# Keys in three chunks of 128 and a rest of 64 instead of four chunks of 112, in an attention and SwiGLU kernel

## The chip, the cores and the metric

The kernel runs on one core of one Trainium2 chip. The time is the device time of one launch in microseconds (us), and the median of several runs is given. Engines are named as the profile names them: PE is TensorE with its matmuls, PEld its weight loads, DVE VectorE, ACT ScalarE, POOL GpSimd. A trailing q marks an engine's own queue of issues.

## The reference

Attention over 8 sequences of 448 tokens and 12 heads of 64, whose result, rearranged to 3584 x 768, goes through a SwiGLU block. All in float32; only the weights of the second block arrive as float64.

```python
def rmsnorm(x, g):
    return x / np.sqrt(np.mean(x * x, axis=-1, keepdims=True) + 1e-06) * g
q_n, k_n = rmsnorm(q, g_q), rmsnorm(k, g_k)              # (8, 12, 448, 64)
scores = (1 / np.sqrt(64)) * np.matmul(q_n, k_n.transpose(0, 1, 3, 2))
attn = np.exp(scores - np.max(scores, axis=-1, keepdims=True))
attn = attn / (np.sum(attn, axis=-1, keepdims=True) + 1e-09)
x = np.matmul(attn, v)  # -> transposed to (3584, 768)
xn = rmsnorm(x, rms_g)
g, val = xn @ w_gate, xn @ w_val                          # (3584, 1536) each
return (g / (1 + np.exp(-g)) * val) @ w_out               # (3584, 768)
```

## The kernel before

The kernel works through 48 pairs of heads, g = 0 to 47, six for each sequence. The keys of a pair lie in NT = 4 chunks of P = 112 tokens, and the scores are held transposed: keys on the partitions, the 448 queries along the row. Four steps on PE belong to a pair.

`turn` transposes the four chunks, both heads side by side (112 rows, 128 columns), so that head 0 lies on partitions 0 to 63 and head 1 on 64 to 127:

```python
def turn(g, i):                      # i = 0: the normalized q, i = 1: k
    ...
    ps = (ps_m if todo else ps_f).tile([128, 512], F32, name="tr", ...)
    for t in range(NT):
        nc.tensor.transpose(ps[:, t * P:(t + 1) * P], src[:, t * 2 * D:(t + 1) * 2 * D], ident[0:P, 0:P])
```

`score` multiplies the keys of one chunk by the queries. The two heads use the two row halves of the array and run at the same time, and ACT makes the exponentials:

```python
def score(g, cs):
    for c in cs:
        for j in range(2):
            r = slice(j * D, (j + 1) * D)
            ps = sc[c, j] = ps_s.tile([128, 512], F32, name="sc", tag="s")
            nc.tensor.matmul(ps[0:P, 0:S], lhsT=qkT[r, 1, c * P:(c + 1) * P], rhs=qkT[r, 0, :], start=True, stop=True)
    for (c, j), ps in sc.items():
        e = st["e", g, c, j] = e_pool.tile([P, S], F32, name="e")
        nc.scalar.activation(e, ps[0:P, 0:S], ACT.Exp, scale=rs[:, n:n + 1])
```

`values` multiplies the exponentials by v, one head on each column half, and `sums` does the same with ones in place of v, for the denominators. For the first seven pairs, g = 0 to 6, PE sums all chunks itself (`direct`); later POOL adds the chunks up first and PE sums one tile per head:

```python
def values(g):
    av = st["av", g] = ps_m.tile([128, 512], F32, name="av", tag="m")
    for c in range(NT):
        for j in range(2):
            nc.tensor.matmul(av[j * D:(j + 1) * D, 0:S], lhsT=vt[:, j, c, :], rhs=st["e", g, c, j],
                             start=(c == 0), stop=(c == NT - 1))

def sums(g):
    den = ...
    terms = [[st["e", g, c, j] ...]] if direct(g) else [[st["es", g, j] for j in range(2)]]
    for i, pair in enumerate(terms):
        for j, term in enumerate(pair):
            nc.tensor.matmul(den[j * D:(j + 1) * D, 0:S], lhsT=ones[0:P, :], rhs=term, ...)
    ...   # reciprocal of den; x = av * reciprocal, on DVE
```

The PSUM banks come from three pools: four for scores, one for `av`, three for the matmuls of the second block. The transposes take one of these three in the early part and the one of `av` later on. Pairs 1 to 6 run back to back. From pair 7 on, an attention block is set between stretches of the second block's matmuls (`ff`, always the full 128 x 128 array), which `fill` issues:

```python
if g < NG:
    pe(lambda: score(g, (0, 1)))
pe(lambda: values(g - 1))
...
pe(lambda: sums(g - 1))
...
    pe(lambda: score(g, (2, 3)))
...
fill(); squares(g + 2, 0); squares(g + 2, 1)
pe(lambda: turn(g + 1, 0)); fill(); pe(lambda: turn(g + 1, 1)); fill()
```

## Time and profile before

| | before |
|---|---|
| median of 3 runs | 1627.66 us (1627.48 to 1628.2) |
| span of the profiled run, granted clock | 1625.3 us, 0.999 |
| first matmul of the second block starts | 95.8 us |
| from there to the end | 1529.5 us |
| one attention block in the steady part | 7.31 us |
| one turn (four transposes) | 0.385 us |

The first two rows are as measured. The others are differences of starts in PE's timeline. That is the way to read PE: it is busy 99% of the span and the ends of its matmuls are modelled, but a start is where work really begins, and from one group's start to the next one's start nothing is lost or counted twice. The lines that carry this are in the prediction.

### The profile page before, as it was taken

What the parts mean: (1) busy time and instruction counts of PE and PEld (TensorE: products, weight loads), DVE (VectorE), ACT (ScalarE), POOL (GpSimd) and SP (SyncE); (2) the same over time, 40 slices, a digit from 0 to 9 for tenths busy, and PEclk for the clock granted to TensorE, in tenths of its full rate; (3) what the DMA queues carried; (4) which work ended last, traced back from release to release, by engine and by line L of the source; (5) the groups of instructions that cost most, each with busy time, mean ns of one, the idle gap of its engine ahead of it and who ended that gap; (6) DMA issues with size and microseconds to landing.
All of it is one profiled execution on the core that took longest, in us unless ns stands there. A gap on an engine that the chain in (4) does not pass through costs nothing.

```text
span 1625.3 us, 21571 instructions
## 1 busy us (share of the span) xinstructions
PE 1608.9 (99%) x7376; PEld 1139.7 (70%) x7376; DVE 871.2 (54%) x1425; ACT 500.3 (31%) x975; POOL 632.2 (39%) x569
## 2 busy tenths in 40 slices
PE   8999999999999999999999999999999999999998
PEld 4444445678855888568865788658786588969974
DVE  6989898487842555335572354624565234433431
ACT  7856563232222332232232222322332123100110
POOL 7777776343523434244334323434343223100000
PEclk9999999999999999999999999999999999999999
DMA  8756674666855555565544655466454453557651
GB/s 223 208 176 200 183 219 134 217 222 200 267 183 154 164 154 156 166 197 154 155 120 131 201 155 147 120 215 194 130 163 132 147 176 108 152 182 239 175 148 45
DMA packets 249036, 276.83 MB, mean 170 GB/s; under 512 B 66644, under 2 KB 245844, under 8 KB 248916
## 3 DMA queue, kind: packets, MB, share of 16 engines
q1 hardware_dynamic: 248596, 275.34, 56.7%
q8 instruction: 61, 1.00, 0.3%
q14 instruction: 59, 0.48, 0.1%
q10 hardware_dynamic: 320, 0.00, 0.0%
HBM read 235.93 MB, written 39.32 MB: 169 GB/s over the span
## 4 chain that ended last, share of the span: by engine, by line
PE 91%; DVE 5%; DMA 2%; ACT 1%; issue 0%; POOL 0%; SPq 0%; DVEq 0%; ACTq 0%; POOLq 0%
PE ff L797 41%; PE ff L991 21%; PE sc L476 9%; PE av L501 9%; PE den L512 3%; PE ff L892 3%; PE ff L1022 2%; PE tr L461 2%; DVE top L646 1%; DVE top L645 1%; DVE rd L520 1%; DVE top L644 1%; DMA raw<-in_moe_w_out_dram 0%; ACT e L480 0%; PE rb L558 0%; DMA raw<-in_moe_w_val_dram 0%
## 5 line engine op out<-in xcount | busy, mean ns | idle before, releaser
L797 PE MATMUL ff<-x,w 128*128 128x224 f32 x1770 | 359.3, 353 | 0.8 <-DVE u L809 0.8
L797 PEld LDWEIGHTS ff<-x,w 128*128 128x128 f32 x1770 | 332.2, 190 | 9.8 <-issue 6.7
L797 PE MATMUL ff<-xs,w 128*128 128x224 f32 x1326 | 272.3, 353 | 0.4 <-DVE cc L809 0.4
L480 ACT ACTIVATE e<-sc,rs 112x448 f32<-112x448 f32 x384 | 212.1, 638 | 190.2 <-PE sc L476 185.2
L486 POOL TENSOR_TENSOR es<-e 112x448 f32<-112x448 f32 x82 | 95.3, 1184 | 436.1 <-ACT e L480 436.0
L797 PEld LDWEIGHTS ff<-xs,w 128*128 128x128 f32 x1326 | 248.6, 190 | 6.1 <-issue 5.3
L490 POOL TENSOR_TENSOR es<-es,e 112x448 f32<-112x448 f32 x164 | 185.9, 1144 | 85.4 <-ACT e L480 78.9
L991 PE MATMUL ff<-w,h 128*128 128x384 f32 x600 | 203.4, 488 | 0.0
L520 DVE RECIPROCAL rd<-rd 128x448 f32<-128x448 f32 x41 | 121.1, 2953 | 135.9 <-ACT rd L519 135.9
L476 PE MATMUL sc<-qkT 64*112 64x448 f32 x768 | 176.7, 562 | 1.6 <-DVE qkT L466 0.8
L991 PEld LDWEIGHTS ff<-w,h 128*128 128x128 f32 x600 | 112.3, 190 | 78.6 <-issue 4.7
L501 PE MATMUL av<-e,vt 112*64 112x448 f32 x768 | 154.9, 545 | 0.0
L444 POOL TENSOR_TENSOR rs<-ms,mhalf 112x16 f32<-112x16 f32 (+1 forms) x50 | 143.7, 2874 | 4.2
L476 PEld LDWEIGHTS sc<-qkT 64*112 64x112 f32 x768 | 68.8, 172 | 93.2 <-issue 69.5
L991 PE MATMUL ff<-w,so 128*128 128x384 f32 x338 | 116.7, 488 | 2.0 <-DVE y L952 2.0
L501 PEld LDWEIGHTS av<-e,vt 112*64 112x64 f32 x768 | 50.8, 136 | 95.8 <-issue 73.9
L1022 PE MATMUL ff<-x,w 128*128 128x448 f32 x288 | 112.0, 542 | 0.0
L809 DVE TENSOR_TENSOR cc<-ff,u 128x448 f32<-128x448 f32 x84 | 52.3, 623 | 93.3 <-PE ff L797 93.0
L991 PEld LDWEIGHTS ff<-w,so 128*128 128x128 f32 x338 | 63.2, 190 | 46.5 <-DVE y L952 3.9
L427 DVE TENSOR_REDUCE ms<-sq 112x8 f32<-112x512 f32 x96 | 61.3, 678 | 52.0 <-ACT sq L424 51.7
L682 POOL TENSOR_TENSOR w<-top,raw 128x384 int32<-128x384 int32 x72 | 78.0, 1097 | 28.3 <-DVE top L646 13.4
L1022 PEld LDWEIGHTS ff<-x,w 128*128 128x128 f32 x288 | 53.3, 190 | 50.9 <-issue 49.0
(104 smaller groups left out, 1676.2 us busy)
## 6 DMA issues: line engine op xcount, KB each, us to landing
w<-kept SPq DMA_DIRECT2D x480, 192.0 KB, 3.2
w<-kept_o SPq DMA_DIRECT2D x290, 192.0 KB, 2.8
kept<-w SPq DMA_DIRECT2D x94, 192.0 KB, 3.7
top<-kept SPq DMA_DIRECT2D x72, 192.0 KB, 3.0
qk<-in_q_dram SPq DMA_DIRECT2D x48, 224.0 KB, 3.6
qk<-in_k_dram SPq DMA_DIRECT2D x96, 112.0 KB, 3.5
vt<-in_v_dram SPq DMA_DIRECT2D x48, 224.0 KB, 2.8
raw<-in_moe_w_gate_dram SPq DMA_DIRECT2D x24, 384.0 KB, 4.7
```

What stands on the lines that cost most here:

```text
L427: nc.vector.tensor_reduce(out=ms[:, i * n:(i + 1) * n], in_=sq.rearrange("p (n d) -> p n d", d=D), axis=AX_X, op=ALU.add)
L444: nc.gpsimd.tensor_tensor(st["rs", g][:, cols], ms, mhalf[0:P, cols], ALU.pow)
L476: nc.tensor.matmul(ps[0:P, 0:S], lhsT=qkT[r, 1, c * P:(c + 1) * P], rhs=qkT[r, 0, :], start=True, stop=True)
L480: nc.scalar.activation(e, ps[0:P, 0:S], ACT.Exp, scale=rs[:, n:n + 1])
L486: nc.gpsimd.tensor_tensor(es, st["e", g, 0, j], st["e", g, 1, j], ALU.add)
L490: nc.gpsimd.tensor_tensor(es, es, st["e", g, c, j], ALU.add)
L501: nc.tensor.matmul(av[j * D:(j + 1) * D, 0:S], lhsT=vt[:, j, c, :], rhs=st["e", g, c, j], start=(c == 0), stop=(c == NT - 1))
L520: nc.vector.reciprocal(rd, rd)
L682: nc.gpsimd.tensor_tensor(data(key).bitcast(I32), top, lo, ALU.add)
L797: nc.tensor.matmul(bank[:, w * HT:(w + 1) * HT], lhsT=wt[:, c * 128:(c + 1) * 128], rhs=x[:, c, :], start=onto is None and w == c == 0, st ...
L991: nc.tensor.matmul(ps, lhsT=a, rhs=data(("wo", b, name, c)), start=first and c == 0, stop=c == NFP - 1, skip_group_check=True)
L1022: nc.tensor.matmul(bank[w][:, 0:S], lhsT=data(key)[:, c * 128:(c + 1) * 128], rhs=st["x", 0, half][:, c, :], start=half == c == 0, stop=ha ...
```

## The change

112 rows use 7/8 of the array's rows. The change takes keys in three full chunks of 128 and a rest of 64 (3 x 128 + 64 = 448). A rest needs only a quarter of the array: 64 rows by 64 columns. Two heads' score rests and two heads' value rests are four such quarters, and the intent is that they run side by side, so that a pair takes 3 + 3 + 1 units of streaming instead of 4 + 4. For this a head's rest is written to the other head's half (`across`), and the score rests of pair g are issued together with the value rests of pair g - 1.

The core of the diff; cut are the loads of q and k (two and three per pair instead of one and two, and two more for v), POOL's adds and powers, the stores of the output, and the order of the first seven pairs. There, in pairs 2 to 6, the turns stand ahead of the values before and after the change, but only one chunk of scores goes ahead of them now instead of two:

```diff
+NK, REST = 3, S - 3 * 128
+    qks = [qk_pool.tile([128, 2, 2 * NT * D], F32, name=f"qk{i}") for i in range(4)]
+    for t in qks:
+        nc.vector.memset(t[REST:128, 0].rearrange("p (h n) -> p h n", h=2)[:, :, NK * D:], 0.0)
+        nc.vector.memset(t[REST:128, 1, 2 * NK * D:], 0.0)
+    def own(j):
+        return slice(j * D, (j + 1) * D)
+    def across(j):
+        return own(1 - j)
 ...
     def turn(g, i):
         for t in range(NT):
-            nc.tensor.transpose(ps[:, t * P:(t + 1) * P], src[:, t * 2 * D:(t + 1) * 2 * D], ident[0:P, 0:P])
+            n = 128 if t < NK else REST
+            nc.tensor.transpose(ps[:, t * 128:t * 128 + n], src[0:n, t * 2 * D:(t + 1) * 2 * D], ident[0:n, 0:n])
 ...
+    def rests(g):
+        if g < NG:
+            qkT = st["qkT", g]
+            ps = ps_s.tile([128, 512], F32, name="sc", tag="s")
+            for j in range(2):
+                nc.tensor.matmul(ps[across(j), 0:S], lhsT=qkT[own(j), 1, NK * 128:S], rhs=qkT[own(j), 0, :], start=True, stop=True)
+        if g:
+            vt, e = st["v", g - 1], st["e", g - 1, "rest"]
+            av = st["av", g - 1] = ps_m.tile([128, 512], F32, name="av", tag="m")
+            for j in range(2):
+                nc.tensor.matmul(av[own(j), 0:S], lhsT=vt[across(j), 2 * NK * D:], rhs=e[across(j), :], start=True, stop=False, ...)
+            if direct(g - 1):
+                den = ...      # the same with ones[across(j), :] for vt
 ...
-        if g < NG:
-            pe(lambda: score(g, (0, 1)))
+        pe(lambda: (rests(g), score(g, (0,)) if g < NG else None))
         pe(lambda: values(g - 1))
 ...
         pe(lambda: sums(g - 1))
 ...
-            pe(lambda: score(g, (2, 3)))
+            pe(lambda: score(g, (1, 2)))
```

## The prediction

> **What bounds the kernel now.** I read four views in this order: the page's busy shares, its chain of work that ended last, the groups by form, and the timeline of the matmul engine, because each narrows the one before. First the page:
>
> ```profile
> PE 1608.9 (99%) x7376; PEld 1139.7 (70%) x7376; DVE 871.2 (54%) x1425; ACT 500.3 (31%) x975; POOL 632.2 (39%) x569
> ...
> PE 91%; DVE 5%; DMA 2%; ACT 1%; issue 0%; POOL 0%; SPq 0%; DVEq 0%; ACTq 0%; POOLq 0%
> ```
>
> The matmul engine (PE) is busy 99% of the span and makes 91% of the chain that ended last. Its ends are modelled, so I checked with starts: in the stretch from 300 us on it is one matmul stream with waits of a microsecond at most. So a microsecond of PE work taken out or put in is a microsecond of time, and what ACT, POOL or DMA gain counts only where PE waits for them. The groups by form name the work that the change touches:
>
> ```profile
> L476 PE MATMUL sc<-qkT 64*112 64x448 f32 x768 | 176.7, 562 | 1.6 <-DVE qkT L466 0.8 <-ACT qkT L464 0.7
> L501 PE MATMUL av<-e,vt 112*64 112x448 f32 x768 | 154.9, 545 | 0.0
> L461 PE MATMUL tr<-ident,qn 112*128 112x112 f32 x192 | 26.8, 261 | 2.4 <-POOL qn L448 2.4
> ```
>
> "64*112" is rows by columns of the array. A float32 matmul leaves two records: 768 records are 384 matmuls, eight for each of 48 pairs of heads. PE waited 1.6 us in all before the scores and 0.0 before the values. One pair in the steady part, from the timeline of PE (start, duration, work):
>
> ```profile
> 617.59 2.43 PE L797 MATMUL ff<-x,w 128*128 128x224 f32 x12
> 619.86 2.43 PE L797 MATMUL ff<-xs,w 128*128 128x224 f32 x12
> 622.23 1.76 PE L476 MATMUL sc<-qkT 64*112 64x448 f32 x8
> 623.92 3.23 PE L501 MATMUL av<-e,vt 112*64 112x448 f32 x16
> 626.98 0.92 PE L512 MATMUL den<-es,ones 112*64 112x448 f32 x4
> 627.83 1.78 PE L476 MATMUL sc<-qkT 64*112 64x448 f32 x8
> 629.54 2.54 PE L797 MATMUL ff<-x,w 128*128 128x224 f32 x12
> 631.91 2.43 PE L797 MATMUL ff<-xs,w 128*128 128x224 f32 x12
> 634.18 2.43 PE L797 MATMUL ff<-x,w 128*128 128x224 f32 x12
> 636.46 0.55 PE L461 MATMUL tr<-ident,qn 112*128 112x112 f32 x4
> 636.84 2.45 PE L797 MATMUL ff<-x,w 128*128 128x224 f32 x12
> ```
>
> Three numbers come from the differences of starts. (a) Streaming: 12 records of 224 columns take 2.27 us where nothing changes (617.59 to 619.86), so 0.189 each and about 0.376 for a record of 448 columns, 0.753 for such a matmul. The values' 16 records take 3.06 us (623.92 to 626.98), eight record times and 0.05: the two heads, on the two column halves, run at the same time. So I count in units: one unit is a pair of matmuls side by side, 0.753 us. (b) A change of shape: the 12 records before the scores take 2.37 instead of 2.27, and the 12 after them 2.37 again (629.54 to 631.91). Scores of two units take 1.69 us, not 1.51. So leaving one shape costs about 0.09 (the drain), and entering 128 or 112 columns another 0.09 to 0.10 (first weights not loaded ahead); entering 64 columns costs 0.05. Values to sums, the same shape, costs nothing more. (c) The transposes between ff work, 112*128, show none of it: 634.18 to 636.46 is 2.28, and the four take 0.38. 112 rows and 128 rows are the same shape to the array, 64 rows are not.
>
> **What the Trainium skill says.** "TensorEngine Tiling (Array Packing)", Key Properties: tiles load weights and multiply in parallel, but "Changing tiling mode (not just tile) drains the TensorE". The trace agrees, at 0.09 a drain. The same page, 64×64 Mode (4 tiles), ties a tile to its partitions: SBUF 0-63 to PSUM 64-127 is tile 2, SBUF 64-127 to PSUM 0-63 is tile 8. No instruction of the kernel before uses this mode. "PSUM — Partial Sum Buffer", PSUM bank collisions: row tiles must not write the same bank and quadrant at once. The two rests share a bank but not a quadrant, so by that page they may run together; no run here shows it yet. "FP8 and Floating Point Precision", TensorE Precision Notes: true FP32 is four passes; 448 columns in 0.753 us fit that at 2.4 columns a ns.
>
> **The change, part by part.**
>
> *Score and value streaming: 0.* Before, a pair of heads has 4 units of scores and 4 of values. After, 3 and 3, and the rests. The intent is that the four rest matmuls lie on four quarters and cost one unit, which would make 7 of 8. But follow the operands. Scores of head 0 read rows 0-63 and write partitions 64-127: tile 2. Scores of head 1: rows 64-127 to 0-63, tile 8. Values of head 0 read the other half, rows 64-127, and write 0-63: tile 8. Values of head 1: tile 2. So both pairs want the same two quarters, and the other two stay empty. The rests cost two units, and 3 + 3 + 2 is 8 as before. The 7 early pairs that sum directly on PE have 3 + 1 units of sums for 4: again none saved.
>
> *Order of shapes in a steady pair: +0.15 us.* Before, PE goes ff, scores, values and sums, scores, ff: four changes. After: ff, rests (64*64), scores (64*128), values and sums (128*64), scores, ff: five. The block before is 1.69 + 3.06 + 0.85 + 1.71 = 7.31. After: rests 0.05 + 1.51 + drain 0.09 = 1.65, scores 0.75 + 0.10 + 0.09 = 0.95, values 2.31, sums 0.85, scores 1.70: 7.46.
>
> *The transposes: +0.37 us each, the largest term.* A turn has three of 128 rows now and one of 64 rows. Columns streamed are 3 x 128 + 64 = 448, as 4 x 112 were, so 0.38 us stays. But the last has 64 rows and 128 columns, the form of the scores, not that of its neighbours. I take it to change the mode twice: in, 0.09 drain and 0.10 weights; out, 0.09 and 0.09. That is 0.37 for a turn, and two turns a pair: +0.74.
>
> *Sum of the steady part.* Pairs 7 to 47, some 40 with both turns: 40 x (0.15 + 0.74) = +36 us, all on PE, which never waits there.
>
> *The first seven pairs, about +1.* The two pairs shown by the windows take 11.31 us on PE, with DVE busy 10.8 and 11.1 of it. There scores run 16 records in 4.24 us instead of 3.2, as they wait for PSUM banks that ACT has to empty; spreading the scores takes away this 1.05. New: three more changes in the order of the rests, values and sums (about 0.5) and three by the turns (0.55). PE comes out near 11.3, the vector engine could not go under 11, so -1 to +3 us for six pairs.
>
> *Off the path.* ACT runs 7 exponentials for 8 in a pair, 0.5 us less, at 31% busy: nothing. POOL has six adds as before and one short power: nothing. DMA moves the same bytes; packets of 1024 bytes of q and v become 768 and 256, 1344 become 1664 a pair, +15,000 on 249,036; eight loads a pair are issued for four. The profile shows no wait of PE on these. The stores of the output come in fewer pieces, off the path too.
>
> *Start: +0.5 to +1.* Eight fills of the unused halves ahead of the first loads, more loads to issue (0.4 to 0.6 us each on the queue), a power more before the first exponential of the rest, against one exponential less.
>
> Sum: 36 + 1 + 1 = 38, so 1627.7 + 38 is about 1665 us.
>
> **Rivals.** First, *the four rests do run at once*, as intended: then 48 x 0.753 = 36 us of streaming is saved and, with the terms above, the time is about 1629. Against it stand the partitions of the operands; for it only the intent. If the turns also cost nothing, 1593. Second, *the 64-row transpose does not change the mode*, or its drain is hidden: then only the 0.15 and the ends remain, 6 + 2, and the time is about 1636. Nothing in the trace has a transpose of 64 rows; for the drain speaks that scores with the same rows pay it on each entry. Third, *the rests of two heads do not overlap*, because they write one bank from two row tiles: two units more, 48 x 1.5 = 72 us on top, near 1735. The page on PSUM speaks against it. Fourth, *DVE or DMA becomes the bound* in the stretch of weight conversion (81 to 285 us, DVE 80 to 97% busy): PE has more work now, so the others get slack; this could only swallow some of the added cost, by a few us, as PE waits 1.6 us there now.
>
> **Range and chances.** I give the transposes' mode change about 70%, and its size 25 to 34 us. That holds the time from 1652 to 1675. The second rival pulls to 1636, so the low end goes there; noise at the start and in the early pairs sets the top at 1682. The 2% mark is 1660.2, below my middle but inside the range, so: slower by over 2% 0.58, within 2% 0.38, faster by over 2% 0.04.
>
> **What would show it.** In the timeline of PE after: a turn that takes 0.7 to 0.8 us from its first start to the next ff start and lengthens the ff group before or after it (right), or 0.38 (wrong). Rests whose score and value records start one unit apart, not within 0.02 us of each other; the attention block at about 7.45 us. ACT, POOL and DMA shares lower or the same, PE still about 99%. Early pairs at 11.0 to 11.8 us. The prediction is wrong if the turns cost no more than before, if value rests start together with score rests, or if a wait of PE on ACT, DVE or DMA of over 5 us in total appears.

## The result

| | before | after |
|---|---|---|
| median | 1627.93 us (4 runs) | 1676.12 us (4 runs, 1675.45 to 1678.09) |
| ratio (95%) | | 1.0298 (1.028 to 1.0316): slower |
| span of the profiled run, granted clock | 1625.3 us, 0.999 | 1673.6 us, 0.996 |

A ratio here is the mean time of one kernel's fast runs over the mean of the other's fast runs of the same rounds, so it is not quite the ratio of the quoted medians. The result is correct. The change costs 48.2 us where 38 were predicted, inside the range.

The chain of work that ended last, on the page of the changed kernel; the shares are of the span, and a shape is not told apart in it:

```profile
PE 80%; DVE 2%; DMA 2%; issue 0%; POOL 0%; ACT 0%; SPq 0%; DVEq 0%; ACTq 0%
```

PE is still all but alone on it. The shares add up to 84%: the chain, laid out in order of time, could be followed back to 241.5 us only, so it says nothing about the early part. The groups by form of the changed kernel show what is new on PE, with count, busy time, mean of one, and PE's idle time before the group:

```profile
L502 PE MATMUL sc<-qkT 64*128 64x448 f32 x576 | 139.5, 579 | 3.7 <-ACT e L541 2.9 <-DVE qkT L492 0.8
L526 PE MATMUL sc<-qkT 64*64 64x448 f32 x192 | 47.3, 570 | 0.8 <-ACT qkT L490 0.7
...
L487 PE MATMUL tr<-ident,qn 64*128 64x64 f32 x48 | 13.2, 274 | 0.0
```

576 + 192 score records are the 768 of before: the number of matmuls is the same. The transposes of the rest are a form of their own, 64*128, as the prediction said they would be. What a form costs is not in this view, since matmuls that overlap and matmuls that do not have the same mean; that is in the starts. One steady pair in PE's timeline of the changed kernel:

```profile
650.79 0.97 PE L526 MATMUL sc<-qkT 64*64 64x448 f32 x4
651.60 0.92 PE L531 MATMUL av<-e,vt 64*64 64x448 f32 x4
652.45 1.02 PE L502 MATMUL sc<-qkT 64*128 64x448 f32 x4
653.40 2.48 PE L549 MATMUL av<-e,vt 128*64 128x448 f32 x12
655.70 0.92 PE L562 MATMUL den<-es,ones 128*64 128x448 f32 x4
656.55 1.80 PE L502 MATMUL sc<-qkT 64*128 64x448 f32 x8
658.28 2.54 PE L848 MATMUL ff<-x,w 128*128 128x224 f32 x12
...
662.93 2.43 PE L848 MATMUL ff<-x,w 128*128 128x224 f32 x12
665.20 0.70 PE L487 MATMUL tr<-ident,qn 128*128 128x128 f32 x4
665.82 2.54 PE L848 MATMUL ff<-x,w 128*128 128x224 f32 x12
668.20 0.85 PE L597 MATMUL msx<-ones,ss 128*112 128x1 f32 x8
```

The score rests start at 650.79 and the value rests 0.81 later, the first scores 0.85 after that: two units, one after the other. The block from 650.79 to 658.28 is 7.49 us, where it was 7.31. The turn runs from 665.20 to 665.82, 0.62 us instead of 0.38, and the 12 `ff` records after it take 2.38 (665.82 to 668.20), where 12 between two `ff` groups take 2.27. (The line of a turn names the shape of its first transposes only.)

The whole of PE, cut into kinds of work by starts and summed, in us; the columns of three experiments are used further down:

| work on PE | before | after | full turn | alternating | both |
|---|---|---|---|---|---|
| until the first `ff` matmul | 95.8 | 105.3 | 104.2 | 103.4 | 101.4 |
| `ff` | 1187.2 | 1196.3 | 1191.2 | 1196.6 | 1191.3 |
| turns (80 from here on) | 31.0 | 51.6 | 36.9 | 51.3 | 36.6 |
| scores | 137.4 | 109.7 | 110.6 | 109.2 | 110.1 |
| score and value rests | – | 66.9 | 66.9 | 37.4 | 37.5 |
| values | 127.5 | 94.5 | 94.5 | 94.5 | 94.5 |
| sums | 35.1 | 38.0 | 39.2 | 40.1 | 40.5 |
| norm of x | 11.3 | 11.4 | 11.4 | 11.4 | 11.5 |
| span | 1625.3 | 1673.6 | 1654.9 | 1644.0 | 1623.2 |

After the first `ff` matmul the change costs 38.9 us (1529.5 to 1568.4): turns 20.6, `ff` 9.1, and the attention work 9.1 (300.0 to 309.1). Before that point it costs 9.5 us, where some 2 were predicted.

These 9.5 have three places. **The start**: the scores of pair 1 begin at 20.72 instead of 16.09, +4.6. ACT's first lines with data, of the kernel before:

```profile
4.01 0.63 ACT L424 ACTIVATE sq<-qk 112x512 f32<-112x512 f32 x1 [1.73 <-DMA qk<-in_q_dram]
```

and of the changed kernel:

```profile
6.26 1.15 ACT L445 ACTIVATE sq<-qk 128x512 f32<-128x512 f32 x2 [3.84 <-DMA qk<-in_k_dram]
```

The first squares start 2.25 us later. The clock differs too: in the changed kernel it is at half from 10.72 to 17.54 us, and before the change it was full from 4.48 us on. The score rests of pair 0 take 1.69 us there (12.74 to 14.43), where 0.80 is usual. How much of the 4.6 us the clock makes, no run here settles. **Pairs 1 to 6** take 2.4 us more in all. **The hand-over** from pair 6 to the second block takes 16.61 us instead of 14.12 to 14.19, some 2.4 more. Here is that stretch, with busy time and number of instructions of PE, PEld, DVE, ACT, POOL, then granted clock, DMA share and GB/s, before:

```profile
81.66:95.78 14.12, 14.12 (x72) 6.21 (x73) 10.31 (x13) 7.94 (x16) 12.19 (x11) 1.00 0.63 196
```

and after:

```profile
88.64:105.25 16.61, 14.63 (x70) 5.87 (x68) 7.23 (x10) 7.38 (x14) 9.69 (x11) 0.90 0.54 159
```

PE waits 1.98 us in it (16.61 less 14.63), and its clock averages 0.90. PE's timeline of the changed kernel there:

```profile
92.54 1.71 PE L531 MATMUL av<-e,vt 64*64 64x448 f32 x4 [1.98 <-issue]
93.98 1.76 PE L536 MATMUL den<-e,ones 64*64 64x448 f32 x4
95.67 1.19 PE L502 MATMUL sc<-qkT 64*128 64x448 f32 x4
```

and DVE's timeline of the changed kernel at the same time:

```profile
88.82 2.96 DVE L566 RECIPROCAL rd<-den 128x448 f32<-128x448 f32 x1 [1.67 <-PE den L562]
91.81 0.62 DVE L577 TENSOR_TENSOR x<-av,rd 128x448 f32<-128x448 f32 x1
```

There is one PSUM bank for `av`. The value rests of pair 6 must write it, and DVE frees it with the product that ends at 92.43, behind a reciprocal of 2.96 us. The value rests start 0.11 us later. "issue" in the brackets means that the profile found no releaser; the two views side by side show it. Before, the values stood behind a whole score group, which covered this time. After the wait PE's clock is at half for about 3.4 us: the value rests take 1.44 us from start to start (92.54 to 93.98) and the sums' rests 1.69, instead of 0.75 to 0.85. The clock's part can be read from the experiment own below: it has the same order and the same wait of 1.98 us here, but no half clock, and takes 14.97 us for the stretch (88.59 to 103.56). So about 1.6 of the 2.4 us come with the half clock, which follows this wait in four of the eleven profiles that have it.

### The profile page after: what moved, and what is told of

Same layout as the page of the kernel before. It is cut to its first block, busy times and chain, and to the rows that moved or that the text cites. A ratio compares the mean times of both kernels' runs of the same rounds, so it can differ in the third digit from the quotient of the medians.

```text
span 1673.6 us, 21741 instructions
## 1 busy us (share of the span) xinstructions
PE 1649.7 (99%) x7376; PEld 1143.5 (68%) x7376; DVE 874.7 (52%) x1433; ACT 478.7 (29%) x927; POOL 658.0 (39%) x617
## 4 chain that ended last, share of the span: by engine, by line
PE 80%; DVE 2%; DMA 2%; issue 0%; POOL 0%; ACT 0%; SPq 0%; DVEq 0%; ACTq 0%
PE ff L848 39%; PE ff L1046 20%; PE sc L502 5%; PE av L549 5%; PE ff L943 3%; PE tr L487 2%; PE sc L526 2%; PE av L531 2%; PE den L562 2%; DMA w<-kept_o 1%; DVE w L805 0%; PE ff L1077 0%; DMA w<-kept 0%; PE rb L609 0%; DVE rd L570 0%
## 5 line engine op out<-in xcount | busy, mean ns | idle before, releaser
L513 POOL TENSOR_TENSOR es<-e 128x448 f32<-128x448 f32 x82 | 94.1, 1147 | 598.4 <-ACT e L506 595.2
L506 ACT ACTIVATE e<-sc,rs 128x448 f32<-128x448 f32 x288 | 162.2, 633 | 70.3 <-PE sc L502 69.2
L465 POOL TENSOR_TENSOR rs<-ms,mhalf 128x16 f32<-128x16 f32 (+1 forms) x50 | 143.4, 2869 | 4.2
L502 PE MATMUL sc<-qkT 64*128 64x448 f32 x576 | 139.5, 579 | 3.7 <-ACT e L541 2.9
L549 PE MATMUL av<-e,vt 128*64 128x448 f32 x576 | 118.8, 548 | 0.0
L502 PEld LDWEIGHTS sc<-qkT 64*128 64x128 f32 x576 | 54.4, 188 | 86.8 <-issue 73.7
L515 POOL TENSOR_TENSOR es<-es,e 64x448 f32<-64x448 f32 x82 | 94.9, 1157 | 6.4
L514 POOL TENSOR_TENSOR es<-es,e 128x448 f32<-128x448 f32 x82 | 94.3, 1150 | 6.4
L448 DVE TENSOR_REDUCE ms<-sq 128x8 f32<-128x512 f32 x96 | 61.3, 678 | 53.8 <-ACT sq L445 53.8
L549 PEld LDWEIGHTS av<-e,vt 128*64 128x64 f32 x576 | 37.1, 136 | 76.2 <-issue 74.9
L1077 PEld LDWEIGHTS ff<-x,w 128*128 128x128 f32 x288 | 53.3, 190 | 51.6 <-issue 49.0
```

Source lines behind the costliest of these rows:

```text
L448: nc.vector.tensor_reduce(out=ms[:, i * n:(i + 1) * n], in_=sq.rearrange("p (n d) -> p n d", d=D), axis=AX_X, op=ALU.add)
L465: nc.gpsimd.tensor_tensor(st["rs", g][:, cols], ms, mhalf[:, cols], ALU.pow)
L502: nc.tensor.matmul(ps[:, 0:S], lhsT=qkT[r, 1, c * 128:(c + 1) * 128], rhs=qkT[r, 0, :], start=True, stop=True)
L506: nc.scalar.activation(e, ps[:, 0:S], ACT.Exp, scale=rs[:, n:n + 1])
L513: nc.gpsimd.tensor_tensor(es, st["e", g, 0, j], st["e", g, 1, j], ALU.add)
L514: nc.gpsimd.tensor_tensor(es, es, st["e", g, 2, j], ALU.add)
```

## The experiments

All twelve gave correct results. Times are medians of four or five runs, with the kernel before in the same rounds. A difference to the changed kernel compares runs of different rounds (the experiments ran on three chips); the medians of the kernel before in these differ by up to 1.2 us, so such a difference is good to 1 or 2 us.

### Full turn: the last transpose with 128 rows

Part of the change undone: the fourth transpose takes all 128 rows (the unused half is zeros) and stays in the shape of its neighbours.

```diff
-            n = 128 if t < NK else REST
-            nc.tensor.transpose(ps[:, t * 128:t * 128 + n], src[0:n, ...], ident[0:n, 0:n])
+            nc.tensor.transpose(ps[:, t * 128:(t + 1) * 128], src[:, ...], ident)
```

> The changed kernel with one edit: the fourth transpose of a turn takes all 128 rows and 128 columns of identity (the lower rows are zeros), so that a turn never leaves the 128x128 mode. Theory (mode changes cost): the turn's run goes from 623 ns to about 440 (four times 107 to 110), the first record after it loses its 0.09 us, so some 0.27 us for each of 80 turns in the steady part: -22 us, and -0 to -3 in the early pairs: 1650 to 1655 us against 1676. Rival (the turn is dearer because of its three 128-column transposes, or by waits, not by the mode): the edit adds 64 columns to each turn, so +0.05 us x 94 = +5 us: about 1681.

Measured: 1655.49 us, ratio to before 1.016 (1.0143 to 1.0177), 20.6 less than the changed kernel. PE's timeline of this kernel:

```profile
657.40 2.43 PE L847 MATMUL ff<-x,w 128*128 128x224 f32 x12
659.67 0.60 PE L486 MATMUL tr<-ident,qn 128*128 128x128 f32 x4
660.11 2.44 PE L847 MATMUL ff<-x,w 128*128 128x224 f32 x12
662.38 0.86 PE L596 MATMUL msx<-ones,ss 128*112 128x1 f32 x8
```

The turn takes 0.44 us (659.67 to 660.11) though it streams 64 columns more than the changed one's 0.62, and the `ff` group after it takes 2.27 again (660.11 to 662.38). In the table, turns fall by 14.7 and `ff` by 5.1. So the 64 rows cost these 20 us. That it is a change of mode is read from the starts: in the changed kernel the transposes of one turn start at 665.20, 665.31, 665.42 and 665.62 and the next `ff` record at 665.82, so the longer steps are those into and out of the 64-row one; here all four steps are 0.11.

### Alternating: rests of odd pairs on swapped halves

The disputed cost taken away by itself. In every second pair a head's rest stays on its own half, so that the score rests of pair g and the value rests of pair g - 1 lie on all four quarters.

```diff
+    def swap(g):
+        return g % 2
+    def on(g, j):
+        return own(j ^ swap(g))
 # the score rest; v's load, the adds, the scale column of the exponential likewise with on(g, j)
-                nc.tensor.matmul(ps[across(j), 0:S], lhsT=qkT[own(j), 1, NK * 128:S], ...)
+                nc.tensor.matmul(ps[on(g, j), 0:S], lhsT=qkT[own(j), 1, NK * 128:S], ...)
 # the value rest, and the sums' rest likewise
-                nc.tensor.matmul(av[own(j), 0:S], lhsT=vt[across(j), 2 * NK * D:], rhs=e[across(j), :], ...)
+                nc.tensor.matmul(av[own(j), 0:S], lhsT=vt[on(g - 1, j), 2 * NK * D:], rhs=e[on(g - 1, j), :], ...)
```

> The changed kernel with one edit: pairs with an even number keep a head's rest on its own half, odd ones on the other half, so that the score rests of a pair and the value rests of the pair before lie on four different quarters. Results stay right. Theory (in the changed kernel both pairs of rests ask for the same two quarters, and that alone makes them two units): value records start within 0.02 us of score records, the rests take 0.9 us instead of 1.65, 41 x 0.75 = -31 us in the steady part and up to -4 in the early pairs: 1641 to 1645 us. Rival (four quarters do not run at once for float32, or the array takes only two streams): no change, 1674 to 1678.

Measured: 1646.71 us, ratio 1.0109 (1.0092 to 1.0126), 29.4 less than the changed kernel, a little over the 1641 to 1645 expected. PE's timeline of this kernel:

```profile
638.89 0.59 PE L533 MATMUL sc<-qkT 64*64 64x448 f32 x2
638.90 0.59 PE L538 MATMUL av<-e,vt 64*64 64x448 f32 x2
639.32 0.54 PE L533 MATMUL sc<-qkT 64*64 64x448 f32 x2
639.33 0.54 PE L538 MATMUL av<-e,vt 64*64 64x448 f32 x2
639.80 1.02 PE L509 MATMUL sc<-qkT 64*128 64x448 f32 x4
```

Score and value rests start 0.01 us apart, and all four are done in 0.91 us (638.89 to 639.80), where the changed kernel takes 1.66 (650.79 to 652.45). That is the unit of 0.75 the change was after. The shared quarters, not the idea of quarters, stood in its way.

### Own: every rest on its own half

The rival to "two rests on one quarter": that the crossing to the other half is what costs. The edit of alternating, but in every pair a head's rest stays on its own head's half, so nothing crosses and two rests again want one quarter.

```diff
     def swap(g):
-        return g % 2
+        return 0
```

> Control for the alternating one: every pair keeps a head's rest on its own half, so both pairs of rests lie on the diagonal quarters instead of the other two. Theory (only sharing a quarter counts, not which quarter): no change, 1674 to 1678 us, rests 1.65 us. Rival (the crossed quarters are slower in themselves): the rests get shorter, and the time falls by up to 31 us.

Measured: 1672.68 us, ratio 1.0266 (1.0249 to 1.0283). PE's timeline of this kernel:

```profile
647.99 0.97 PE L533 MATMUL sc<-qkT 64*64 64x448 f32 x4
648.79 0.92 PE L538 MATMUL av<-e,vt 64*64 64x448 f32 x4
```

The rests are one after the other again, 0.80 apart. Which half they use does not matter, only that two want the same. From the first `ff` matmul on this kernel takes 1567.4 us, the changed one 1568.4. Its other 1.7 us lie in the early part (103.6 instead of 105.3), where it shows no stretch of half clock near 92 us; its profiled run came out below what was expected mostly for that reason.

### Both: full turn and alternating together

> The full 128-row fourth transpose and the alternating halves together. Theory (two separate costs on the matmul engine, each paid in full): the two gains add, 1676.1 - 20.6 - 29.4 = 1626 us, as fast as the kernel before (1628 to 1629) within 0.3%. Rival (the early pairs or the weight conversion on the vector engine take over as the bound once the matmul engine has less to do): 1631 to 1640.

Measured: 1626.07 us, ratio 0.9988 (0.9975 to 1.0002). The two effects add up: by the medians 20.6 + 29.4 = 50.0, and 1676.1 to 1626.1 is 50.1; by the ratios to before, 0.0138 + 0.0189 = 0.0327, and 0.0310 measured. So they are separate causes. With them the kernel is level with the one before, not faster. The table tells where the unit saved is spent: after the first `ff` matmul this kernel needs 1521.8 us, 7.7 less than before, with 17.4 less of attention work (300.0 to 282.6), 5.6 more of turns and 4.1 more of `ff`; until then it needs 5.6 more.

### Fills later: the eight fills behind the first loads

The first suspect for the start: the fills of the unused halves stand ahead of `ones` on DVE, and ACT's first work waits for `ones`.

```diff
-    for t in qks:          # at the head of the kernel
-        nc.vector.memset(...); nc.vector.memset(...)
+    for t in qks:          # after the constants
+        nc.vector.memset(...); nc.vector.memset(...)
```

> The changed kernel with its eight fills of the unused halves moved behind the fill of the ones. First scores now start at 12.74 us against 9.91 before the change, the second pair's at 20.72 against 16.09. Theory (the fills hold up the fill of the ones, ACT's first square waits for it, and the small loads of the gains that ACT issues after it hold up the squares): first square of q at 4.0 to 4.5 us instead of 6.26, first scores near 10.5, total -2 to -3 us. Rival (the start is late because a pair has eight loads to issue instead of four, about 0.6 us each): first square 0 to 0.5 us earlier and total -0.5 us or less.

Measured: 1675.45 us, ratio 1.0278 (1.026 to 1.0295), against 1.0298: no gain that the intervals show. They are too wide to exclude the theory's 2 to 3 us (the four runs go from 1672.59 to 1677.53, and the profiled one is the slowest); the profile shows no gain. ACT's timeline of this kernel:

```profile
4.49 0.63 ACT L442 ACTIVATE sq<-qk 128x512 f32<-128x512 f32 x1 [2.22 <-DMA qk<-in_q_dram]
...
14.47 0.63 ACT L442 ACTIVATE sq<-qk 128x512 f32<-128x512 f32 x1 [1.54 <-DMA qk<-in_k_dram]
15.00 0.62 ACT L538 ACTIVATE e<-sc,rs 128x448 f32<-128x448 f32 x1
```

The first square starts at 4.49, near the 4.01 of before, and PE's first scores at 10.97 instead of 12.74. But the first exponential runs at 15.00, where it ran at 14.85 in the changed kernel: ACT takes its work in order, and ahead of it stand squares of the third pair, which wait for a load. What was gained is lost at the next thing in the queue. The clock is a second cause that this run does not separate: it is at half from 9.01 to 26.08 us here, and the 12 score records after the first rests take 6.29 us (12.66 to 18.95), where the changed kernel takes 4.05 (14.43 to 18.48).

### Start: third pair's squares behind the first exponentials

Fills later, the third pair loaded before v, and its squares behind pair 0's exponentials.

```diff
-    load_v(0)
     load_pair(2)
+    load_v(0)
-    squares(2, 0)
-    squares(2, 1)
 ...
             pe(lambda: rests(0))
             pe(lambda: score(0, (0, 1, 2)))
+            squares(2, 0)
+            squares(2, 1)
```

> The changed kernel with only the start altered: the eight fills behind the fill of the ones, the loads of the third pair ahead of the loads of v, and the squares of the third pair behind the exponentials of the first on ACT. The run with the fills alone had first scores 1.8 us earlier and no gain, as ACT then waited until 14.5 us for the third pair's loads before the first exponential. Theory (the start is set by loads issued one by one at 0.6 us each and by squares that stand ahead of the exponentials in ACT's queue): first exponential near 12.5 us instead of 14.85, second pair's scores near 18 instead of 20.7, total -2 to -3.5 us: 1672.5 to 1674. Rival (the early pairs are paced by DVE and POOL, so an earlier start is given back before the first ff): 0 to -1 us.

Measured: 1674.89 us, ratio 1.0291 (1.0277 to 1.0305): within the noise of the changed kernel. The first exponential now starts at 12.81, but the scores of pair 1 only at 20.31 (20.72 in the changed kernel). DVE's timeline of this kernel:

```profile
18.35 1.28 DVE L445 TENSOR_REDUCE ms<-sq 128x8 f32<-128x512 f32 x2 [7.06 <-ACT sq L442]
19.55 0.62 DVE L489 COPY qkT<-tr 128x448 f32<-128x448 f32 x1
```

The copy of pair 1's keys, which these scores need, stands behind the reduces of the third pair's squares, which now come late. DVE sat idle for 7.06 us before them. The wait went from ACT's queue to DVE's.

### Hand-over: two chunks of scores ahead of the rests of pair 7

```diff
+        if g == NPAIR + 1:
+            pe(lambda: (score(g, (0, 1)), rests(g)))
+        else:
             pe(lambda: (rests(g), score(g, (0,)) if g < NG else None))
 ...
-            pe(lambda: score(g, (1, 2)))      # for g == NPAIR + 1
+            pe(lambda: score(g, (2,)))
```

> The changed kernel with one edit in the pair at which the early order ends (pair 7): its scores of chunks 0 and 1 stand ahead of the rests. There the value rests wait 1.98 us for the one PSUM bank of the values, which the vector engine frees only after its 2.95 us reciprocal, and the clock is throttled afterwards. Theory: the wait is filled with scores, -1.5 to -2.5 us: 1673.6 to 1674.6. Rival (it is not on the path that sets the end, the vector engine is): no change, 0 to -0.5.

Measured: 1677.48 us, ratio 1.0304 (1.029 to 1.0318): no gain. PE's timeline of this kernel:

```profile
94.85 1.76 PE L526 MATMUL sc<-qkT 64*64 64x448 f32 x4 [2.64 <-ACT e L506]
```

The rests of pair 7 want a score bank themselves, and all four are taken by the two chunks. The exponential that frees one stands on ACT behind a square of x, which waits for DVE. PE waits 2.64 us for it instead of 1.98 for the `av` bank, and the clock is at half for 6.8 us, from 93.72 on.

### All: both, start and hand-over together

> All four edits together: full transposes, alternating halves, the altered start, the altered pair 7. If they add: 1626 - 3 - 2 = 1619 to 1623 us, faster than the kernel before by 0.3 to 0.6%. If the early part is paced by the vector engine and POOL: 1625 to 1630.

Measured: 1628.78 us, ratio 1.0007 (0.9993 to 1.0021): 2.7 us more than both alone by the medians, with intervals that overlap. The gain expected if the parts add up is missed; the time lies in the other expectation. The trace shows the wait of the hand-over experiment again (2.66 us for ACT's exponential), and the scores of pair 1 begin at 20.89 us, no earlier than the 20.39 of both.

### Start, second try: the third pair's squares behind pair 1's turns

On top of both: the fills later, the third pair loaded before v, and `squares(2, ...)` issued behind the turns of pair 1 instead of ahead of them.

> The version with full transposes and alternating halves (1626.1), plus a second try at the start. In the first try the exponentials did come earlier (12.8 and 14.5 us), but the vector engine's copy of the second pair's keys then stood behind the sums of the third pair's squares (18.35 us), so the second pair's scores started at 20.3 all the same. Here the squares of the third pair stand behind the turns of the second. Theory (the start is a queue order, and with this one out of the way it is shorter): second pair's scores near 18 us instead of 20.4, 1626.1 - 2.3 = 1624. Rival (the early pairs run at a pace set elsewhere and give it back): 1625.5 to 1627.

Measured: 1629.96 us, ratio 1.0011 (0.9997 to 1.0024). The scores of pair 1 begin at 18.12 us instead of 20.39. But then the turn of pair 2 waits 4.14 us for POOL's normalized q, which hangs on those squares, until 27.35, and the clock is at half from 25.24 to 32.07. A miss of the same kind, above both expectations.

### Late turns: the early turns behind the values

On top of both: in pairs 2 to 6 the turns stand behind the rests and values, so that PE does not wait for POOL's q. (The text says "put back"; in the kernel before, the turns stood ahead of the values in these pairs too, and behind them in pair 1 alone.)

```diff
-            if g > 1:
-                pe(lambda: turn(g + 1, 0))
-                pe(lambda: turn(g + 1, 1))
             pe(lambda: rests(g))
             pe(lambda: values(g - 1))
-            if g == 1:
-                pe(lambda: turn(g + 1, 0))
-                pe(lambda: turn(g + 1, 1))
+            pe(lambda: turn(g + 1, 0))
+            pe(lambda: turn(g + 1, 1))
```

> The version with full transposes and alternating halves, with the two turns of the early pairs 2 to 6 put back behind the values. There PE waits up to 0.68 us a pair for POOL's normalised q. Theory (that wait paces the early pairs): the pair takes about 11.0 us instead of 11.32, 1626.1 - 1.5 = 1624.6. Rival (the one PSUM bank of the values, freed 3.9 us after the sums end by the vector engine, takes its place): 1625.5 to 1629, with the wait ahead of the value rests.

Measured: 1632.42 us, ratio 1.0021 (1.0007 to 1.0035), 5 to 6 us more than both alone (by the ratios and by the medians): the rival named the right wait, and its 1625.5 to 1629 was too low. PE's timeline of this kernel:

```profile
33.50 0.97 PE L537 MATMUL av<-e,vt 64*64 64x448 f32 x4 [1.13 <-issue]
```

Every early pair now waits 1.13 to 1.20 us for the one `av` bank and takes 12.28 to 12.35 us instead of 11.32. So the place of the turns in the change has a reason: they fill the time in which DVE frees the bank.

### Second try and late turns on top of both

> Both of the last edits together. If each pays: 1622 to 1623 us. If the early part is paced by the vector engine: 1625 to 1628.

Measured: 1636.04 us, ratio 1.0047 (1.0033 to 1.0061). The trace shows both waits, 4.02 us at the turn of pair 2 and 1.12 to 1.19 in each of five pairs. They add up (9.6 us over both by the ratios, where 3.7 and 5.4 were measured alone), so the reading of each holds; the version is no use and lies above both expectations.

### The early edits on the changed kernel itself

Fills later, the third pair loaded before v, its squares behind pair 0's exponentials and pair 1's turns, and late turns, on the changed kernel without the other two edits.

> The same two edits on the changed kernel itself, without the full transposes and the alternation. Of its 48 us, 9.5 come before the first matmul of the feed-forward part, where 2 were predicted. If the queue order at the start and the early place of the turns make that excess, the time falls by 3 to 5 us, to 1671 to 1673. If it is paced elsewhere: 1675 to 1678.

Measured: 1684.42 us, ratio 1.034 (1.0326 to 1.0355), 7 to 8 us more than the changed kernel and outside both expectations. The trace has the wait for the `av` bank in each pair (1.13 to 1.20), early pairs of 12.5 us, and a wait of 2.93 us at the turn of pair 2. Its first `ff` matmul starts at 110.39, 5.1 later than in the changed kernel.

## Why the prediction was right or wrong

**PE as the only bound: right in the steady part.** The kinds of work on PE add up to the 38.9 us by which that part is longer. In the early part it was not the only one, as below.

**No streaming saved, as two rests want one quarter: right, and shown** by alternating (four quarters, -29.4 us) together with own (one half for both again, rests 0.80 apart). The third rival, that the rests of two heads do not overlap, is answered by the changed kernel itself: their four records would take 1.5 us one after the other and take 0.81 (650.79 to 651.60). The first rival in the prediction would have been right with other operands; its 36 us for 48 pairs compare with 29.4 measured. In the table the rests fall by 29.5, close to 40 x 0.75; some 2 of it goes to scores that wait longer for the rest's exponential to free a bank (5.0 us, where it was 2.9), which shows in the row of the sums, and 2 come in the early part.

**Order of shapes, 0.15 a pair: right.** In the median block 7.488 less 7.315 is 0.173, 6.9 us for 40 pairs. With 1.3 us more of waits (2.9, where 1.6 were) this is most of the +9.1 of the attention work, where 6 stood in the sum.

**The 64-row transpose costs extra time: right, and shown** by the full turn; that it is the change of mode is read from the starts. Its size was 0.37 and is 0.33: 0.24 in the turn (0.385 to 0.62) and 0.09 in the `ff` group after it. For 80 turns that is 26 us, where 29.6 stood in the sum; the table has 20.6 in turns and some 5 in `ff`. The other 4 us of `ff` are there in the version of both too (1191.3 against 1187.2). About 2.3 of them are waits for DVE (1.5 and 2.0 us before the two main `ff` groups, where they were 0.8 and 0.4). What the rest is, I did not settle.

**The early part: wrong.** The step that failed is "the first seven pairs, about +1" with "start: +0.5 to +1": 2 us in the sum, 9.5 measured, so 7.5 of the 10 us by which the sum was short. (The steady part, 38.9 where 36 stood, has the other 3.) The prediction counted PE's work there and took waits as gone. Its range for the six pairs, -1 to +3, does hold the 2.4 measured. Its start was too small, 4.6 where 0.5 to 1 stood, as it did not ask what order ACT, DVE and POOL have there; and it had no term for the hand-over, 2.4, as it did not ask what frees the single `av` bank when less PE work goes ahead of the values. Nor does DVE's busy time bound an early pair at 11: it is 9.99 of 11.57 us in one of the changed kernel (45.00 to 56.57). Full turn and alternating together bring the five pairs back to 11.32 us each, as before, with less work on PE than before. In that trace the value rests of these pairs start 0.06 to 0.15 us after DVE's product ends; before, the values started 1.3 to 1.4 us after it. This says that there the loop through the reciprocal, the product and the bank sets the pace, not PE. It is read from the trace, and not shown by a run with a second bank for `av`: the pools hold four, one and three, and I did not take one from another. For the start and the hand-over, four attempts to move one piece of work (fills later, start, hand-over, second try) each removed the wait that they aimed at, and another wait, or a longer stretch of half clock, came in its place. So the place of these 7 us is measured. Their cause stays open, but for the 1.6 us of half clock at the hand-over: moving any one of these pieces of work alone gained nothing that could be measured.

**Waits over 5 us in all** was a sign named for a wrong prediction. PE's waits that the trace puts down to ACT, DVE or DMA come to 9.9 us, and were 6.4; with the 1.98 us of "issue" that is 5.6 more, so the sign just came true. The chief terms of the sum held all the same.

**Two sums of the prediction** do not come out. Its first rival with free turns would be near 1600 us, not 1593, since the 6 us for the order of shapes were left out. And its terms (25 to 34 us for the turns, -1 to +3 for the early pairs) give 1658 to 1672, not 1652 to 1675. The measured 1676 lies above either; only the top set wide for the start and the early pairs, where the miss then was, holds it.

**The best version** is both, 1626.07 us against 1627.67 for the kernel before in the same rounds. Its interval (0.9975 to 1.0002) holds 1, so it is level, not better.

## What to carry to other kernels

When work is packed on parts of the array, write down for every matmul which rows it reads and which partitions it writes: in this kernel, two that shared a quarter ran one after the other, and that alone decided 29 us of 48. A short piece with another number of rows between full-size matmuls can cost more than the columns it saves; here padding it with zeros to the full shape took 20 us off. And before reordering work around a single buffer or an in-order engine, find what releases it: here every reorder of the early part that was tried gained nothing.

## What the Trainium skill lacked or had wrong

- "TensorEngine Tiling (Array Packing)", Key Properties, says that a change of mode drains and that tiles work in parallel, and gives no cost for either; nor does it say that a transpose of 64 rows is such a change. Here a mode change cost, as read from the starts, about 0.09 us for the drain and 0.05 to 0.10 for first weights, 0.33 us for one 64-row transpose between full ones. Four float32 matmuls of 448 columns on four quarters took 0.91 us, and 1.66 when two shared each of two quarters. The same page's Gotcha 1 says that row tiles cannot access one PSUM bank at the same time. The rests of the two heads come from two row tiles and go to two halves of one bank; both were done 0.80 us after their start, where one after the other would take 1.5, with correct results.
- "TensorE: Matmul & The Clock Gate", Part 1, puts the return to the half clock after one idle window of about 3.4 us, which runs freely. Here an idle time of 1.98 us was followed by half the clock for about 3.4 us, and one of 2.64 us went with 6.8 us of it. A reader who counts only gaps over 3.4 us would miss these; but the length of the gap alone does not decide: in seven other profiles (own and both among them) the same wait of 1.98 or 1.99 us was followed by no half clock. The page tells of shorter idle times only where they come often, between groups of matmuls.
- No page of those read says what a single wait for a PSUM bank looks like in the profile; "Perfetto Trace Analysis" names only gaps that repeat as a sign of too few buffers. Here it stood as "issue", 1.98 us, and was found only by laying the engine that frees the bank beside it.
